# A SwiGLU feed-forward kernel: the last 96 rows of the down-projection in row quarters of the array

## The chip, the cores and the metric

The kernel runs on one core of one Trainium2 chip. A core has a matmul engine (TensorE, an array of 128 x 128 cells), VectorE, ScalarE, GpSimd, SyncE and 16 DMA engines. The metric is the device time of one execution in microseconds (us). The kernel before takes 121.23 us, the median of three runs (120.81 to 121.36).

## The reference

x has 2048 tokens of 512 numbers; the weights are 512 x 1376, 512 x 1376 and 1376 x 512; all is bf16.

```python
g = silu(x @ w_gate)
u = x @ w_up
return (g * u) @ w_down
```

1376 = 10 x 128 + 96. The hidden dimension therefore has ten full blocks of 128 and a rest of 96.

## The kernel before

Everything stays in the core's own memory: x transposed (`xT_sb`), both input weights (`w_sb`), w_down (`wd_sb`), and h = silu(gate) * up, transposed, hidden rows on partitions (`hT_sb`, eleven blocks; block 10 holds the last 96 rows). A planner at lines 116 to 211 writes down all groups of matmuls in order, and gives each group the next of eight accumulator banks in turn. The engines wait for each other by counters: TensorE counts groups (`s_P`), ScalarE and VectorE count their operations (`s_A`, `s_D`).

The order on TensorE (`on_tensor`):

- six warming matmuls (L290) and eight transposes of the first rows of x (L297);
- for each of four chunks of 512 tokens, ten pairs of groups G and U (gate and up for one hidden block, four matmuls each of 128 x 128 weights and 512 tokens, L282). ScalarE takes silu of G, VectorE multiplies it by U and writes h (L242). After the ten pairs follows one group X (L316), four matmuls with 64 columns of gate and 64 of others, which gives 32 of the last 96 rows of h;
- two groups Y (L327), each for two chunks: sixteen matmuls in all whose weights have 64 columns, in pairs, one in the left and one in the right half of the array's columns. They give the other 64 of the last 96 rows, which VectorE multiplies and writes to `hT_sb[0:64, 10]`;
- sixteen output tiles of 128 tokens, groups O (L344): each is eleven matmuls into one bank, ten over 128 hidden rows and one over the last 96. The last tile is in two banks, of 384 and 128 output columns, so that its first part can be copied and stored earlier.

VectorE copies each finished output bank to one of three buffers `o_sb` (L246; ScalarE copies the 384 columns of the last tile, L235), and SyncE stores the buffer (L218). SyncE also issues nearly all loads, at the start (lines 99 to 112); the stores stand behind them in its queue. A wait of SyncE holds back all that follows on it. ScalarE has nothing to do between the last silu and the copy of the last tile.

A group may start when the bank's former group, eight groups before, has been read (`free`). A load that has to be there is waited for once (`need`).

Of the kernel before, what the change touches and what calls it, by code (L numbers as in the profile page):

```python
# [6 lines left out]
BF16 = mybir.dt.bfloat16  # L7
# [5 lines left out]
def bass_standalone__swiglu_ffn__prompt_kernel(nc, x, w_gate, w_up, w_down, out):  # L13
    _, S, D = x.shape
    F = w_gate.shape[1]
    P = 128
    KD = D // P
    NFF = F // P
    NFT = NFF + 1
    F_LAST = F - NFF * P  # L20
    SC = 512
    NSC = S // SC
    TPC = SC // P
    NST = S // P
    LASTA = 384
    HT = SC // 2
    NB = 8
    NSG = 4
    NOS = 3
    assert D == 512 and S % SC == 0 and KD == 4 and F_LAST == 96 and NSC % 2 == 0  # L30

    xf = x[0]
# [8 lines left out]
    with ExitStack() as es:  # L41
        sb = lambda name, shape, dt: es.enter_context(nc.sbuf_tensor(name, shape, dt))
        ps = lambda name, shape, dt: es.enter_context(nc.psum_tensor(name, shape, dt))
        sem = lambda name: es.enter_context(nc.semaphore(name))

        xT_sb = sb("xT_sb", [P, KD, S], BF16)
        w_sb = sb("w_sb", [P, KD, WTOT], BF16)
        wd_sb = sb("wd_sb", [P, NFT, D], BF16)
        hT_sb = sb("hT_sb", [P, NFT, S], BF16)
        adummy = sb("act_dummy", [P, 8], FP32)  # L50
        sg_sb = [sb(f"sg_sb{i}", [P, SC], FP32) for i in range(NSG)]
        sgx_sb = [sb(f"sgx_sb{c}", [P, SC], FP32) for c in range(NSC)]
# [6 lines left out]
        s_P = sem("s_P")  # L59
        s_A = sem("s_A")  # L60
        s_D = sem("s_D")
        s_I = sem("s_I")
        s_out = [sem(f"s_out{i}") for i in range(NOS)]
        loads = {}

        def load_sem(name):
            loads[name] = sem(f"s_{name}")
            return loads[name]
# [23 lines left out]
        def load_up(eng, a, b):  # L92
            load_w(eng, f"wu{a}", w_up, UPH, a * P, min(b * P, F - 32))

        def loads_on_scalar(act):
            load_gate(act, *slabs[0])
            load_up(act, *slabs[0])

        def loads_on_sync(sp):
            for t in range(TPC // 2):  # L100
                sp.dma_start(x0_sb[:, t, :], xf[t * P:(t + 1) * P, :]).then_inc(load_sem(f"t{t}"), 16)
            load_x(sp, "x0b", HT, SC)
            for a, b in slabs[1:]:
                load_gate(sp, a, b)
                load_up(sp, a, b)
            load_w(sp, "wut", w_up, F - (F - 32), F - 32, F)
            for c in range(1, NSC):
                load_x(sp, f"x{c}", c * SC, (c + 1) * SC)
            sp.dma_start(
                wd_sb[:, 0:NFF, :], w_down[0:NFF * P, :].rearrange("(k p) d -> p k d", p=P)  # L110
            ).then_inc(load_sem("wd"), 16)
            sp.dma_start(wd_sb[0:F_LAST, NFF, :], w_down[NFF * P:F, :]).then_inc(load_sem("wdt"), 16)

        groups = []
        n_read = {"A": 0, "D": 0}
# [7 lines left out]
        def add_op(eng, g, **what):  # L125
            n_read[eng] += 1
            op = dict(g=g, at=n_read[eng], **what)
            (act_ops if eng == "A" else dve_ops).append(op)
            g["readers"].append((eng, op["at"]))
            return op  # L130
# [3 lines left out]
        h_ready = {}  # L134
# [18 lines left out]

        y_after = {}
        t_ready = {}

        def plan_x(c):
            g = add_group("X", c=c)
            y0, y1 = yblk(c)
            add_op("A", g, kind="silu", out=sgx_sb[c][96:128, :], src=g["bank"][64:96, :], free=0)  # L160
            a = add_op("A", g, kind="silu", out=sgy_sb[c][y0:y1, :], src=g["bank"][0:64, :], free=0)
            add_op(
                "D", g, kind="mul", out=hT_sb[64:96, NFF, c * SC:(c + 1) * SC],
                a=sgx_sb[c][96:128, :], b=g["bank"][96:128, :], after=a["at"] - 1,
            )
            y_after[c] = a["at"]
# [13 lines left out]
        for t in range(TPC // 2):  # L180
            for half, eng in enumerate("AD"):
                g = add_group("T", t=t, k0=2 * half)
                op = add_op(
                    eng, g, kind="copy", stored=(s_I, 0),
                    out=xT_sb[:, 2 * half:2 * half + 2, t * P:(t + 1) * P],
                    src=g["bank"][:, 0:2 * P].rearrange("p (k t) -> p k t", k=2),
                )
                x0_ready.append((2 * half, eng, op["at"]))
        n_T = len(groups)
# [9 lines left out]
        for t in range(NST):  # L199
            ob = t % NOS  # L200
            need = 16 * n_store[ob]
            halves = [(0, D)] if t < NST - 1 else [(0, LASTA), (LASTA, D)]
            for c0, c1 in halves:
                g = add_group("O", t=t, c0=c0, c1=c1)
                eng = "A" if len(halves) == 2 and c0 == 0 else "D"
                op = add_op(
                    eng, g, kind="copy", out=o_sb[ob][:, c0:c1], src=g["bank"][:, 0:c1 - c0],
                    stored=(s_out[ob], need),
                )
# [3 lines left out]

        def on_sync(sp):
            loads_on_sync(sp)
            for t, c0, c1, ob, eng, n in stores:
                sp.wait_ge(s_A if eng == "A" else s_D, n)
                sp.dma_start(of[t * P:(t + 1) * P, c0:c1], o_sb[ob][:, c0:c1]).then_inc(s_out[ob], 16)  # L218
            for i in range(NOS):
                sp.wait_ge(s_out[i], 16 * n_store[i])  # L220

        def on_scalar(act):
            loads_on_scalar(act)
            act.activation(adummy[:, 0:4], zero_c, ACT.Silu)  # L224
            for op in act_ops:
                act.wait_ge(s_P, op["g"]["at"] + 1)
                if op["kind"] == "silu":
                    if op["free"]:
                        act.wait_ge(s_D, op["free"])
                    fn = ACT.Silu  # L230
                else:
                    if op["stored"][1]:
                        act.wait_ge(*op["stored"])
                    fn = ACT.Copy
                act.activation(op["out"], op["src"], fn).then_inc(s_A, 1)  # L235
# [13 lines left out]
        def on_tensor(pe):  # L249
            landed = set()  # L250

            def need(name):
                if name not in landed:
                    pe.wait_ge(loads[name], 16)
                    landed.add(name)
# [3 lines left out]
            def after(eng, n):  # L259
                if n > read[eng]:  # L260
                    pe.wait_ge(s_A if eng == "A" else s_D, n)
                    read[eng] = n

            def free(g):
                if g["at"] >= NB:
                    for eng, n in groups[g["at"] - NB]["readers"]:
                        after(eng, n)
# [35 lines left out]
            for n0, n1 in ((0, HT), (HT, SC)):  # L303
                for g in groups[n_T:n_T + 2]:
                    gu_matmuls(g, n0, n1)
            for g in groups[n_T + 2:]:
                free(g)
                kind = g["kind"]
                if kind in "GU":
                    gu_matmuls(g, 0, SC)  # L310
                elif kind == "X":
                    c = g["c"]
                    need(f"wg{slab_of[NFF]}")
                    need("wut")
                    for dk in range(KD):
                        ins = pe.matmul(  # L316
                            g["bank"][:, :], lhsT=w_sb[:, dk, XC0:XC0 + P],
                            rhs=xT_sb[:, dk, c * SC:(c + 1) * SC],
                            start=(dk == 0), stop=(dk == KD - 1),
                        )  # L320
                    ins.then_inc(s_P, 1)
                elif kind == "Y":
                    need(f"wu{slab_of[NFF]}")
                    for dk in range(KD):
                        for c in (2 * g["pi"], 2 * g["pi"] + 1):
                            y0, y1 = yblk(c)
                            ins = pe.matmul(  # L327
                                g["bank"][y0:y1, :], lhsT=w_sb[:, dk, YC0:YC0 + 64],
                                rhs=xT_sb[:, dk, c * SC:(c + 1) * SC],
                                start=(dk == 0), stop=(dk == KD - 1),  # L330
                                tile_position=(0, y0), skip_group_check=True,
                            )
                    ins.then_inc(s_P, 1)
                else:
                    t, c0, c1 = g["t"], g["c0"], g["c1"]
                    c = t // TPC
                    need("wd")
                    after("D", h_ready[c])
                    for fk in range(NFT):
                        K = P if fk < NFF else F_LAST  # L340
                        if fk == NFF:
                            need("wdt")
                            after("D", t_ready[c])
                        ins = pe.matmul(  # L344
                            g["bank"][:, 0:c1 - c0], lhsT=hT_sb[0:K, fk, t * P:(t + 1) * P],
                            rhs=wd_sb[0:K, fk, c0:c1], start=(fk == 0), stop=(fk == NFT - 1),
                        )
                    ins.then_inc(s_P, 1)

        nc.gpsimd.affine_select(  # L350
            ident[:, :], ones_w, pattern=[[-1, P]], compare_op=ALU.is_equal, fill=0.0, base=0,
# [34 lines left out]
```

## Time and profile before

| | |
|---|---|
| time of the profiled execution | 121.29 us |
| its span, first to last instruction | 120.0 us |
| median of three runs | 121.23 us |
| TensorE matmuls (L282, L316, L327, L344) in the profile | 328, 16, 16, 187 |
| VectorE copy of an output bank (L246) | 0.69 us |
| ScalarE silu of a bank (L235) | 0.60 us |
| store of a 128 KB output tile, issue to landing | 1.7 us |
| granted TensorE clock | 1.0 |

The span runs from the first instruction to the last, the time of the execution a little more. "Busy" of TensorE is from the start of a matmul to its modelled end; a matmul begins well before its predecessor has ended, so the mean duration of one (379 ns at 512 columns) is longer than the step from start to start, and it is the step that counts for the time. The weight load of a matmul is an instruction of its own (PEld), which in this kernel mostly runs beside the matmul before it.

### The profile page before, as it was taken

How to read it: one execution, taken by the hardware profiler on the slowest of the kernel's cores; microseconds unless marked ns; L12 is line 12 of the kernel's file. 1: busy time of each engine (PE TensorE's matmuls, PEld its weight loads, DVE VectorE, ACT ScalarE, POOL GpSimd, SP SyncE). 2: the span in 40 equal slices, each digit the busy share in tenths (PEclk: the TensorE clock that was granted, in tenths of full speed). 3: DMA queues.
4: the chain of work that ended last, by engine and by line, in shares of the span. 5: the costliest groups of instructions: out<-in, count | busy, mean ns of one | idle time of the engine just before them, and what ended most of it. 6: DMA issues, size and time to landing. Idle time of an engine off the chain costs nothing.

```text
span 120.0 us, 1415 instructions
## 1 busy us (share of the span) xinstructions
PE 117.0 (97%) x561; PEld 53.9 (45%) x561; DVE 44.5 (37%) x66; ACT 31.1 (26%) x53; POOL 0.5 (0%) x5
## 2 busy tenths in 40 slices
PE   7899999999999999999999999999999999999993
PEld 2564444444444444444444444344444444444452
DVE  0224433444434444334444334466233224222420
ACT  3333233262333272333262333230000000000001
POOL 1000000000000000000000000000000000000000
DMA  3999999930000000000000000000211121111112
GB/s 89 231 306 372 287 218 182 302 127 0 0 0 0 0 0 5 0 0 5 0 0 0 0 5 0 0 0 0 87 44 44 52 85 44 44 66 66 44 44 87
DMA packets 17254, 8.51 MB, mean 71 GB/s; under 512 B 10496, under 2 KB 17248, under 8 KB 17248
## 3 DMA queue, kind: packets, MB, share of 16 engines
q1 hardware_dynamic: 16192, 8.16, 25.4%
q10 hardware_dynamic: 1056, 0.26, 1.0%
q8 instruction: 4, 0.07, 0.3%
q14 instruction: 2, 0.02, 0.0%
HBM read 4.49 MB, written 2.10 MB: 55 GB/s over the span
## 4 chain that ended last, share of the span: by engine, by line
PE 97%; ACT 0%; DVE 0%; issue 0%
PE bank L282 58%; PE bank L344 32%; PE bank L316 3%; PE bank L290 2%; PE bank L327 2%; PE bank L297 1%; ACT xT_sb L235 0%; DVE o_sb L246 0%
## 5 line engine op out<-in xcount | busy, mean ns | idle before, releaser
L282 PE MATMUL bank<-xT_sb,w_sb 128*128 128x512 bf16 (+1 forms) x328 | 70.2, 376 | 0.4 <-ACT xT_sb L235 0.4
L282 PEld LDWEIGHTS bank<-xT_sb,w_sb 128*128 128x128 bf16 x328 | 32.2, 98 | 37.7 <-issue 0.6
L242 DVE TENSOR_TENSOR hT_sb<-sg_sb,bank 128x512 bf16<-128x512 f32 x40 | 27.5, 688 | 40.8 <-PE bank L282 37.6
L344 PE MATMUL bank<-wd_sb,hT_sb 128*128 128x512 bf16 (+4 forms) x187 | 38.3, 367 | 0.0
L235 ACT ACTIVATE sg_sb<-bank 128x512 f32<-128x512 f32 x40 | 23.8, 596 | 41.6 <-PE bank L282 41.6
L344 PEld LDWEIGHTS bank<-wd_sb,hT_sb 128*128 128x128 bf16 (+1 forms) x187 | 17.8, 98 | 20.7 <-DVE hT_sb L242 0.4
L246 DVE CAST o_sb<-bank 128x512 bf16<-128x512 f32 (+1 forms) x16 | 10.7, 667 | 25.4 <-PE bank L344 25.3
L235 ACT ACTIVATE o_sb<-bank 128x384 bf16<-128x384 f32 x1 | 0.5, 490 | 38.2 <-PE bank L344 38.2
L316 PE MATMUL bank<-xT_sb,w_sb 128*128 128x512 bf16 x16 | 4.1, 379 | 0.0
L242 DVE TENSOR_TENSOR hT_sb<-sgx_sb,bank 32x512 bf16<-32x512 f32 x4 | 2.8, 692 | 3.5 <-ACT sgx_sb L235 3.5
L290 PE MATMUL bank<-const-bfloat16-1.0 128*128 128x512 bf16 x6 | 2.7, 623 | 0.8 <-PEq L371 0.8
L235 ACT ACTIVATE sgx_sb<-bank 32x512 f32<-32x512 f32 x4 | 2.3, 587 | 4.5 <-PE bank L316 4.5
L242 DVE TENSOR_TENSOR hT_sb<-sgy_sb,bank 64x512 bf16<-64x512 f32 x4 | 2.7, 685 | 0.1
L316 PEld LDWEIGHTS bank<-xT_sb,w_sb 128*128 128x128 bf16 x16 | 1.6, 98 | 1.9
L246 DVE CAST xT_sb<-bank 128x256 bf16<-128x256 f32 x2 | 0.8, 424 | 4.2 <-PE bank L297 4.0
L235 ACT ACTIVATE sgy_sb<-bank 64x512 f32<-64x512 f32 x4 | 2.4, 589 | 0.1
L327 PE MATMUL bank<-xT_sb,w_sb 128*64 128x512 bf16 x16 | 1.9, 382 | 0.0
L224 ACT ACT_TABLE_LOAD x1 | 1.3, 1283 | 1.9 <-issue 1.9
L290 PEld LDWEIGHTS bank<-const-bfloat16-1.0 128*128 128x128 bf16 x6 | 0.7, 133 | 1.9 <-issue 1.9
L327 PEld LDWEIGHTS bank<-xT_sb,w_sb 128*64 128x64 bf16 x16 | 0.8, 109 | 1.0 <-DVE hT_sb L242 0.4
L297 PE MATMUL bank<-ident,x_sb 128*128 128x128 bf16 x8 | 1.2, 309 | 0.0
L297 PEld LDWEIGHTS bank<-ident,x_sb 128*128 128x128 bf16 x8 | 0.8, 133 | 0.8 <-issue 0.5
(7 smaller groups left out, 1.7 us busy)
## 6 DMA issues: line engine op xcount, KB each, us to landing
out_dram<-o_sb SPq DMA_DIRECT2D x15, 128.0 KB, 1.7
wd_sb<-in_w_down_dram SPq DMA_DIRECT2D x1, 1280.0 KB, 6.9
w_sb<-in_w_gate_dram SPq DMA_DIRECT2D x1, 480.0 KB, 5.5
w_sb<-in_w_up_dram SPq DMA_DIRECT2D x1, 448.0 KB, 6.1
w_sb<-in_w_gate_dram SPq DMA_DIRECT2D x1, 384.0 KB, 4.6
w_sb<-in_w_up_dram SPq DMA_DIRECT2D x1, 384.0 KB, 5.1
x_sb<-in_x_dram SPq DMA_DIRECT2D x2, 128.0 KB, 2.5
w_sb<-in_w_gate_dram SPq DMA_DIRECT2D x1, 256.0 KB, 3.9
```

The source lines that it names most:

```text
L224: act.activation(adummy[:, 0:4], zero_c, ACT.Silu)
L235: act.activation(op["out"], op["src"], fn).then_inc(s_A, 1)
L242: ins = dve.tensor_tensor(op["out"], op["a"], op["b"], ALU.mult)
L246: ins = dve.tensor_copy(op["out"], op["src"])
L282: ins = pe.matmul(g["bank"][:, n0:n1], lhsT=w_sb[:, dk, col:col + P], rhs=xT_sb[:, dk, c * SC + n0:c * SC + n1], start=(dk == 0), stop=(dk ...
L290: pe.matmul(banks[NB - 1][:, :], lhsT=ones_w, rhs=ones_m, start=True, stop=True)
L297: ins = pe.matmul(g["bank"][:, i * P:(i + 1) * P], lhsT=x0_sb[:, g["t"], k * P:(k + 1) * P], rhs=ident[:, :], start=True, stop=True,)
L316: ins = pe.matmul(g["bank"][:, :], lhsT=w_sb[:, dk, XC0:XC0 + P], rhs=xT_sb[:, dk, c * SC:(c + 1) * SC], start=(dk == 0), stop=(dk == KD - 1),
L327: ins = pe.matmul(g["bank"][y0:y1, :], lhsT=w_sb[:, dk, YC0:YC0 + 64], rhs=xT_sb[:, dk, c * SC:(c + 1) * SC], start=(dk == 0), stop=(dk == ...
L344: ins = pe.matmul(g["bank"][:, 0:c1 - c0], lhsT=hT_sb[0:K, fk, t * P:(t + 1) * P], rhs=wd_sb[0:K, fk, c0:c1], start=(fk == 0), stop=(fk == ...
```

## The change

The 96-row matmuls of the output tiles are replaced, all but the very last one of 128 columns. The 96 rows are three pieces of 32. For four tiles at once, four matmuls of 32 rows, each in its own quarter of the array's rows and into its own bank, go one after the other: quarter r takes tile r; three such packs make up the 96 rows of four tiles. A matmul in a quarter reads weights and data from the partitions of that quarter, so the rows have to lie in all four quarters:

- `wdr_sb` holds the last 96 rows of w_down four times, by four loads;
- `hr_sb` holds the 32 rows of piece i for tile r on the partitions of quarter r. `spread` issues four DMAs for one piece and one pair of chunks, 24 in all. SyncE issues pieces 2 and 0 (16 DMAs) ahead of all stores, each after a wait for the VectorE multiplies that write them; ScalarE issues piece 1 (8 DMAs) ahead of its only output copy.

The order of the output groups, for each pair of chunks (eight tiles): 40 matmuls of the ten full blocks of four tiles (the banks stay open), the 12 quarter matmuls that close these four banks, the 12 that open the next four, and then the 40 matmuls that finish those, bank by bank. The closing of four banks is told once, by an increment of four. The last 128 columns of the last tile follow by themselves, as before. There are six output buffers instead of three, and the load of the last 96 rows into `wd_sb` brings only the 128 columns that the last group needs.

```diff
-    NOS = 3
+    NOS = 6
+    R = 32
+    NPC = 3
...
+        wdr_sb = sb("wdr_sb", [P, NPC, D], BF16)
+        hr_sb = sb("hr_sb", [P, NSC, NPC, P], BF16)
...
+        def spread(eng, pi, i):
+            for r in range(TPC):
+                tok = slice(2 * pi * SC, (2 * pi + 2) * SC)
+                eng.dma_start(
+                    hr_sb[R * r:R * (r + 1), 2 * pi:2 * pi + 2, i, :],
+                    hT_sb[R * i:R * (i + 1), NFF, tok].rearrange("p (c t) -> p c t", c=2)[:, :, r * P:(r + 1) * P],
+                ).then_inc(s_hr[pi], 16)
...
-            sp.dma_start(wd_sb[0:F_LAST, NFF, :], w_down[NFF * P:F, :]).then_inc(load_sem("wdt"), 16)
+            load_sem("wdr")
+            for r in range(TPC):
+                sp.dma_start(
+                    wdr_sb[R * r:R * (r + 1), :, :], w_down[NFF * P:F, :].rearrange("(i p) d -> p i d", p=R)
+                ).then_inc(loads["wdr"], 16)
+            sp.dma_start(wd_sb[0:F_LAST, NFF, LASTA:D], w_down[NFF * P:F, LASTA:D]).then_inc(load_sem("wdt"), 16)
...
         def on_sync(sp):
             loads_on_sync(sp)
+            for pi in range(NSC // 2):
+                sp.wait_ge(s_D, x_ready[2 * pi + 1])
+                spread(sp, pi, 2)
+            for pi in range(NSC // 2):
+                sp.wait_ge(s_D, t_ready[2 * pi + 1])
+                spread(sp, pi, 0)
             for t, c0, c1, ob, eng, n in stores:
...
             for op in act_ops:
+                if op["g"]["kind"] == "O":
+                    for pi in range(NSC // 2):
+                        act.wait_ge(s_D, t_ready[2 * pi + 1])
+                        spread(act, pi, 1)
...
+            def strips(c, gs, first, last):
+                pe.wait_ge(s_hr[c // 2], 16 * NPC * TPC)
+                for i in range(NPC):
+                    for r, g in enumerate(gs):
+                        c0, c1 = g["c0"], g["c1"]
                         ins = pe.matmul(
-                            g["bank"][:, 0:c1 - c0], lhsT=hT_sb[0:K, fk, t * P:(t + 1) * P],
-                            rhs=wd_sb[0:K, fk, c0:c1], start=(fk == 0), stop=(fk == NFT - 1),
+                            g["bank"][:, 0:c1 - c0], lhsT=hr_sb[R * r:R * (r + 1), c, i, :],
+                            rhs=wdr_sb[R * r:R * (r + 1), i, c0:c1],
+                            start=first and i == 0, stop=last and i == NPC - 1,
+                            tile_position=(R * r, 0), skip_group_check=True,
                         )
-                    ins.then_inc(s_P, 1)
+                return ins
+
+            og = [g for g in groups if g["kind"] == "O"]
+            for pi in range(NSC // 2):
+                ga = og[2 * pi * TPC:(2 * pi + 1) * TPC]
+                gb = og[(2 * pi + 1) * TPC:(2 * pi + 2) * TPC]
+                for g in ga:
+                    free(g)
+                    mains(g, True, False)
+                for g in gb:
+                    free(g)
+                if "wdr" not in landed:
+                    pe.wait_ge(loads["wdr"], 16 * TPC)
+                    landed.add("wdr")
+                strips(2 * pi, ga, False, True).then_inc(s_P, TPC)
+                strips(2 * pi + 1, gb, True, False)
+                for g in gb:
+                    mains(g, False, True).then_inc(s_P, 1)
+            g = og[-1]
+            free(g)
+            mains(g, True, False)
+            need("wdt")
+            after("D", t_ready[NSC - 1])
+            pe.matmul(
+                g["bank"][:, 0:g["c1"] - g["c0"]], lhsT=hT_sb[0:F_LAST, NFF, g["t"] * P:(g["t"] + 1) * P],
+                rhs=wd_sb[0:F_LAST, NFF, g["c0"]:g["c1"]],
+                start=False, stop=True,
+            ).then_inc(s_P, 1)
```

`mains(g, first, last)` issues the ten full-block matmuls of one group, after waiting for `wd` and for the h of the chunk; its `start` and `stop` say whether the bank is opened by its first matmul and closed by its last.

## The prediction

> **What bounds the kernel now.** I read the page first, for the share of each engine, then the chain of work that ended last, then the groups with their shapes kept apart, then the timeline around the two places where the array's shape changes.
>
> The page's first part:
>
> ```profile
> PE 117.0 (97%) x561; PEld 53.9 (45%) x561; DVE 44.5 (37%) x66; ACT 31.1 (26%) x53; POOL 0.5 (0%) x5
> ```
>
> TensorE works in 97% of the span, everything else in under half of it. The chain in order of time (start, length, what; us):
>
> ```profile
> 59.98 17.27 PE bank L282 x80
> 77.24 0.86 PE bank L316 x4
> 78.11 1.85 PE bank L327 x16
> 79.95 38.21 PE bank L344 x187
> 118.16 0.02 issue
> 118.19 0.29 DVE o_sb L246
> ```
>
> The chain hardly leaves TensorE: what shortens or lengthens its stream moves the end one for one. 17.27 / 80 = 0.2159 us is the pace of a 512-column matmul. The 187 matmuls of the down-projection run without a hole at that pace. Its groups, shapes kept apart (busy, mean ns of one):
>
> ```profile
> L344 PE MATMUL bank<-wd_sb,hT_sb 128*128 128x512 bf16 x150 | 34.8, 379 | 0.0
> L344 PE MATMUL bank<-wd_sb,hT_sb 96*128 96x512 bf16 x15 | 5.7, 381 | 0.0
> L327 PE MATMUL bank<-xT_sb,w_sb 128*64 128x512 bf16 x16 | 1.9, 382 | 0.0
> L344 PEld LDWEIGHTS bank<-wd_sb,hT_sb 96*128 96x128 bf16 x17 | 1.7, 98 | 1.8
> L327 PEld LDWEIGHTS bank<-xT_sb,w_sb 128*64 128x64 bf16 x16 | 0.8, 109 | 1.0 <-DVE hT_sb L242 0.4
> ```
>
> A 96-row matmul lasts as long as a 128-row one (381 against 379 ns): a quarter of the array idles in it. The 379 ns are start to modelled end; the next one starts after 216. The 16 half-width matmuls of L327 were busy for 1.9 us together: 8 pairs, not 16 in a row. So two column halves of the array do run side by side here. Row quarters do not occur in this trace.
>
> **What is removed.** Of the 17 matmuls over the last 96 rows, 16 go: fifteen of 512 columns and one of 384. The pace of 384 columns comes from the timeline of TensorE:
>
> ```profile
> 115.58 1.79 PE L344 MATMUL bank<-wd_sb,hT_sb 128*128 128x384 bf16 x10
> ```
>
> The last of these ten starts at 115.58 + 1.79 - 0.33 (its duration) = 117.04, so nine steps took 1.46 us, 0.162 each. Removed: 15 x 0.2159 + 0.162 = **3.40 us**, all on the path.
>
> **What is added on TensorE.** 48 quarter matmuls (32 rows), in 12 packs of four: 3 pieces of 32 rows x 4 sections of four banks. A pack cannot be faster than the 512 columns that each member streams, 0.216 us; if the four did not overlap at all it would be 4 x 0.2159 = 0.864. Nearest row: the pairs of L327. Their first starts at 78.04 and the last ends at 79.95, so it started at 79.57 (382 ns each); of these 1.53 us, 7 x 0.2159 = 1.51 are the steps between eight pairs and 0.02 is how much the second member lags. A pair thus costs one matmul's pace. Four members need four weight loads per pack, where the pair needs two. The nearest row for a dense row of loads is the tail of 128 columns:
>
> ```profile
> 117.59 0.56 PE L344 MATMUL bank<-wd_sb,hT_sb 128*128 128x128 bf16 x7
> ```
>
> (0.56 - 0.22) / 6 = 57 ns for a load with its matmul. Four of those make 0.228 us, hardly above 0.216. I take 0.216: 12 x 0.2159 = **2.59 us**; at 0.228 it is 2.74. The change of matmuls alone is 3.40 - 2.59 = 0.81 us less.
>
> **What the changes of shape cost.** The two closing-and-opening sections stand together, so the array changes to quarters twice and back twice. The trace has one such change each way, into and out of L327's halves:
>
> ```profile
> 77.08 1.03 PE L316 MATMUL bank<-xT_sb,w_sb 128*128 128x512 bf16 x4
> 77.08 0.53 PEld L316 LDWEIGHTS bank<-xT_sb,w_sb 128*128 128x128 bf16 x3
> 77.28 0.69 DVE L242 TENSOR_TENSOR hT_sb<-sg_sb,bank 128x512 bf16<-128x512 f32 x1 [1.04 <-PE bank L282]
> 78.03 0.14 PEld L327 LDWEIGHTS bank<-xT_sb,w_sb 128*64 128x64 bf16 x4 [0.42 <-DVE hT_sb L242]
> 78.04 0.41 PE L327 MATMUL bank<-xT_sb,w_sb 128*64 128x512 bf16 x2
> ...
> 79.88 0.76 PEld L344 LDWEIGHTS bank<-wd_sb,hT_sb 128*128 128x128 bf16 x5 [0.41 <-DVE hT_sb L242]
> 79.89 1.04 PE L344 MATMUL bank<-wd_sb,hT_sb 128*128 128x512 bf16 x4
> ```
>
> The last L316 starts at 77.08 + 1.03 - 0.38 = 77.73; at pace its successor would start at 77.95 and starts at 78.04: 0.09 late. On the way back, 79.57 + 0.216 = 79.79 against 79.89: 0.10 late. The loads tell why: elsewhere a load runs ahead beside the matmul before it; here it starts 0.01 us ahead of its own matmul. The page names VectorE's multiply as what ended the wait, but what the halves wait for is the read of a bank used eight groups before, a multiply three pairs (some 5 us) earlier. So I take the 0.09 and 0.10 as the price of the change of shape: 2 x (0.09 + 0.10) = 0.39 us, plus the lag of a pack's fourth member, 3 x 0.02 per section, 0.12 us in all. Together **0.51 us**. Bounds: nothing, if quarters need no such pause; 0.38 us each (a matmul's whole duration before the next begins), 1.5 us. I stay with 0.1, the only change of shape measured here.
>
> **What the copies of h cost.** 24 small DMAs copy the last 96 rows of h to the four quarters, 16 issued by SyncE, 8 by ScalarE; four loads of the last rows of w_down replace one. The stores queue behind the copies on SyncE. Issue rows of SyncE (start, length):
>
> ```profile
> 19.10 0.58 SPq L109 DMA_DIRECT2D wd_sb<-in_w_down_dram  x1
> 19.73 0.69 SPq L112 DMA_DIRECT2D wd_sb<-in_w_down_dram  x1
> ...
> 118.50 0.38 SPq L218 DMA_DIRECT2D out_dram<-o_sb  x1
> ```
>
> The loads are issued before 25 us and wanted after 80: nothing. The copies for the first two sections: four wait for the multiplies of the X groups, the last of which ends at 78.83 + 0.69 = 79.52, and four more on SyncE for the Y multiplies, at 79.56 + 1.40 = 80.96. (Four for the first pair of the X pieces went long before; here the second pair's stand in front.) Eight issues at 0.38 to 0.69 from 79.5 are done by 82.6 to 85.0; landing takes 1.7 (store) to 2.5 us (small x load) by the page, so 84.3 to 87.5. First wanted: after 40 matmuls, 79.89 + 40 x 0.2159 = 88.53. So it is hidden, with 1 to 4 us to spare. ScalarE issues its eight in a stretch of 38 us in which it waits only for the last tile. What stands behind the waits on SyncE is the first store, and its data now come after 89 us. Later copies have 17 us more.
>
> **Banks and the end.** A section now hands four banks over at once: VectorE needs 4 x 0.69 = 2.8 us for them, in which TensorE runs a section of packs and then the 2.16 us of the next bank; the four banks are wanted again about 8 us later. Six output buffers instead of three let the four copies go without a store between them. The last bank keeps its eleven matmuls of 128 columns and the same copy and store: no change behind TensorE.
>
> **Sum.** -3.40 + 2.59 + 0.51 = -0.30 us. The profiled execution took 121.29 us (span 120.0, 1.3 around it); the median of the three runs is 121.23. 121.29 - 0.30 = 120.99: I forecast **121.0**, 0.2% below the median, inside the 0.5% (0.6 us) that a measurement can tell from no change. With the packs at 0.228 it is 121.1.
>
> One statement speaks against the sum. The Trainium skill, "TensorE: Matmul & The Clock Gate", section "Measured speedup vs the span model", gives four 32-row tiles of 512 columns a speedup of 3.07, not 4. As an estimate from that page, a pack would be 4 x 0.2159 / 3.07 = 0.281 us, twelve 3.38, and the kernel 121.8. The pairs of L327 reach 2.0 here, so I keep the trace's pace; no row here shows quarters.
>
> **Rivals.**
>
> *Quarters change shape for nothing (faster).* If the pause of L327 belongs to halves of columns (their load lasts 109 ns for 64 columns, the full one 98 for 128, so they load otherwise), only the 0.12 us of lag stay: -0.69 us, 120.6; without lag 120.5. Against it: the pause is there in both directions, into and out of the halves.
>
> *The loads of a quarter do not run ahead (slower).* If a load into the quarter that is in use waits for that quarter's matmul, each pack shows the 0.1 us that a load not run ahead costs at the change of shape: 12 x 0.1 = +1.2 us, so 121.29 - 0.30 + 1.2 = 122.2. It makes the kernel slower by over 0.5% from (0.6 + 0.3) / 12 = 75 ns per pack on. Against it: in L327 four loads lie within 0.14 us, ahead of the second pair, and the pairs keep the pace of 0.216. For it: eight loads in flight, not four, and no row of quarters.
> The skill's same page, section "The mechanism", says that a load overlaps a running matmul only where their row groups differ; the pairs of L327 use all rows, and their loads overlap, so the trace does not bear that out here.
>
> *The quarters do not run side by side.* Two at a time: 24 x 0.2159 = 5.18, so +2.3 us, 123.6; one at a time 10.4 us, 128.8. For it only that the trace has no row quarter; it would mean that the packs do not do what they are for.
>
> *Rows of h come late.* With all issues at 0.93 us (the longest issue of a weight load in the trace) eight end at 87.0, land at 89.5, 0.9 us late: 121.9. The short issue rows speak against it, since each copy is small.
>
> **Chances.** Forecast (packs 0.216 to 0.228, pauses near 0.1; 120.8 to 121.4): 0.47. No pause: 0.26. Loads exposed: 0.15. Not side by side: 0.07. Late rows: 0.05. So faster by over 0.5%: 0.26, within: 0.47, slower: 0.27. The range from 120.5 to 122.2 takes in the free and the exposed case and leaves out the not-side-by-side one and the ends of the others.
>
> **What would show it.** Twelve packs with starts 0.216 apart, four members within some 0.06 us; a load that starts just ahead of its matmul and a start about 0.1 us late at each of four places; no wait on a DMA at the first quarter matmul near 88.5 us; the span shorter by 0.3. A step of 0.28 or more between packs makes me wrong upwards, matmuls at pace across the change of shape downwards.

## The result, and the profile after

The changed kernel takes 120.82 us (median of 22 runs, 120.45 to 121.47) where the kernel before, run beside it, takes 121.16. The medians differ by 0.34 us; the ratio is 0.9969, 95% interval 0.9956 to 0.9983. (A ratio compares fast runs alone, here without one slow run of 123.48 us, and is not the plain quotient of the medians.) A second comparison, told below, gave 0.9994 (0.9968 to 1.0020). Both intervals hold 0.2 to 0.3% less, and the second also holds no gain at all. The forecast was 0.2% less, and 121.0 us: 0.18 more than measured, mostly as it was counted from one execution of 121.29. The difference is below the 0.5% that was called the limit of a measurement here, so the traces have to carry the explanation.

The page of the changed kernel, first part, and its chain of work in order of time (start, length, what; us):

```profile
PE 116.1 (97%) x593; PEld 53.0 (44%) x593; DVE 44.0 (37%) x66; ACT 31.1 (26%) x53; POOL 0.5 (0%) x5
```

```profile
77.66 1.85 PE bank L359 x16
79.51 8.74 PE bank L373 x40
88.25 1.41 PE bank L385 x24
89.65 17.37 PE bank L373 x80
107.03 1.40 PE bank L385 x21
108.43 8.77 PE bank L373 x50
117.19 0.07 PE bank L414
117.27 0.02 issue
117.29 0.29 DVE o_sb L278
```

The one piece of 38.21 us (L344) has become six. The two of L385 are the quarter matmuls: 24 in 1.4 us, where 24 in a row would take 5.2 (the chain counts 21 in the second piece; it holds 24 too, three of them of 384 columns). Such a piece, from the change to quarters to the change back, is called a stay. From the start of the first full output matmul to the start of the last matmul, the down-projection took 79.89 to 117.93 before and takes 79.44 to 117.03 now: 38.04 against 37.59, **0.45 us less**. (That it starts 0.45 us earlier as well has nothing to do with the change: the first 88 gate and up matmuls, which are the same, took 17.95 us in one profiled execution and 17.48 in the other, since some of the first ones, of 256 columns, went at half pace in the former, 0.213 us from start to start where 0.109 is usual. A version below that equals the changed kernel up to there took 18.15. That is why spans of single executions, 120.0 and 119.3, are not compared here, but stretches.)

The timeline around the first stay in quarters (start, length, engine, line, in how many):

```profile
87.22 1.03 PE L373 MATMUL bank<-wd_sb,hT_sb 128*128 128x512 bf16 x4
87.44 0.31 PEld L373 LDWEIGHTS bank<-wd_sb,hT_sb 128*128 128x128 bf16 x2
88.17 0.98 PEld L385 LDWEIGHTS bank<-wdr_sb,hr_sb 32*128 32x128 bf16 x24 [0.42 <-issue]
88.18 1.48 PE L385 MATMUL bank<-wdr_sb,hr_sb 32*128 32x512 bf16 x24
89.06 1.89 DVE L278 CAST o_sb<-bank 128x512 bf16<-128x512 f32 x3 [7.11 <-PE bank L385]
89.58 0.98 PEld L373 LDWEIGHTS bank<-wd_sb,hT_sb 128*128 128x128 bf16 x6 [0.42 <-issue]
89.59 1.25 PE L373 MATMUL bank<-wd_sb,hT_sb 128*128 128x512 bf16 x5
```

This is the picture that L327 gave before: at each change of shape the first weight load starts 0.01 us ahead of its own matmul instead of beside the one before it. The last full matmul starts at 87.87, the first quarter at 88.18: 0.312 us where 0.216 is the pace, **0.10 late**. The last quarter starts at 89.28, the next full one at 89.59: 0.306, **0.09 late**. No wait on a DMA stands there; the idle time of the load is "issue".

The end holds what the forecast did not have. The last store is issued at 117.61 and lands 1.5 us later:

```profile
117.61 0.39 SPq L246 DMA_DIRECT2D out_dram<-o_sb  x1
```

```profile
out_dram<-o_sb SPq DMA_DIRECT2D x1, 32.0 KB, 1.5
```

The landing is at 119.11, but the span ends at 119.30. In the kernel before, issue 118.50, landing 120.01, end 120.03. What stands behind the landing are SyncE's closing waits for the output buffers, before and after (how many; shortest, median and longest in ns; first and last start):

```profile
L220 SPq EVENT_SEMAPHORE  x2: 17/522/1027, 118.9 to 119.0; - x2
```

```profile
L248 SPq EVENT_SEMAPHORE  x3: 28/28/28, 119.1 to 119.3; - x3
```

The records join the waits for two buffers in one instruction, and not in the order of the program: before, buffer 1 alone, then 2 with 0; now 3 with 2, 4 with 1, 5 with 0. The last store is from buffer 0 before and from buffer 3 now. So the wait that the last store releases was the last instruction before (1027 ns long, to 120.03), and is the first of three now: they end at 119.16, 119.23 and 119.30. **0.17 us came back at the end**. Sum of the two stretches: -0.45 + 0.17 = -0.28 us.

### The profile page after: what moved, and what is told of

The parts are those of the page before. It is cut to its first block, busy times and chain, and to the rows that moved or that the text cites. A ratio compares the mean times of both kernels' runs of the same rounds, so it can differ in the third digit from the quotient of the medians.

```text
span 119.3 us, 1509 instructions
## 1 busy us (share of the span) xinstructions
PE 116.1 (97%) x593; PEld 53.0 (44%) x593; DVE 44.0 (37%) x66; ACT 31.1 (26%) x53; POOL 0.5 (0%) x5
## 4 chain that ended last, share of the span: by engine, by line
PE 97%; ACT 0%; DVE 0%; issue 0%
PE bank L314 58%; PE bank L373 29%; PE bank L348 3%; PE bank L385 2%; PE bank L322 2%; PE bank L359 2%; PE bank L329 1%; ACT xT_sb L267 0%; DVE o_sb L278 0%; PE bank L414 0%
## 5 line engine op out<-in xcount | busy, mean ns | idle before, releaser
L373 PE MATMUL bank<-wd_sb,hT_sb 128*128 128x512 bf16 (+2 forms) x170 | 35.1, 367 | 0.0
L373 PEld LDWEIGHTS bank<-wd_sb,hT_sb 128*128 128x128 bf16 x170 | 16.0, 98 | 19.2 <-issue 0.8
L278 DVE CAST o_sb<-bank 128x512 bf16<-128x512 f32 (+1 forms) x16 | 10.1, 663 | 25.5 <-PE bank L385 15.8
L385 PE MATMUL bank<-wdr_sb,hr_sb 32*128 32x512 bf16 (+1 forms) x48 | 2.9, 373 | 0.0
L385 PEld LDWEIGHTS bank<-wdr_sb,hr_sb 32*128 32x128 bf16 x48 | 1.1, 93 | 1.7 <-issue 0.8
```

Source lines behind the costliest of these rows:

```text
L278: ins = dve.tensor_copy(op["out"], op["src"])
L373: ins = pe.matmul(g["bank"][:, 0:c1 - c0], lhsT=hT_sb[:, fk, t * P:(t + 1) * P], rhs=wd_sb[:, fk, c0:c1], start=first and fk == 0, stop=la ...
L385: ins = pe.matmul(g["bank"][:, 0:c1 - c0], lhsT=hr_sb[R * r:R * (r + 1), c, i, :], rhs=wdr_sb[R * r:R * (r + 1), i, c0:c1], start=first an ...
```

## The experiments

Theory: the packs run at the pace of one full matmul, and each change of shape stops TensorE for about 0.1 us. Rivals: changes of shape are free, and the late starts have another cause; the loads of the quarters are exposed. Times are medians; ratios are to the kernel before, run on the same chip.

**Two more stays in quarters.**

```diff
-                strips(2 * pi + 1, gb, True, False)
-                for g in gb:
+                mains(gb[0], True, False)
+                strips(2 * pi + 1, gb, True, False).then_inc(s_P, 1)
+                for g in gb[1:]:
                     mains(g, False, True).then_inc(s_P, 1)
```

(and `start` is not set for the first tile of the second section.)

> Each of the two places with quarter matmuls is parted in two by the ten full matmuls of the fifth tile, so that the array changes shape eight times instead of four; number and kind of matmuls stay. Theory (a change of shape stops TensorE for 0.10 us on the way in and 0.09 on the way out, about 0.21 with the slow first steps): two more stays, +0.42 us, 121.2 us, ratio to the kernel before about 1.000. Rival (the late starts belong to something met once per pair of chunks, such as the wait for the copies of h or for the banks, and a change of shape is free): as the changed kernel, 120.8, ratio 0.997.

Measured: 121.29 us, ratio 1.0017 (0.9998 to 1.0035). Its chain:

```profile
88.22 0.76 PE bank L385 x12
88.98 2.26 PE bank L373 x10
91.25 0.76 PE bank L385 x12
```

The down-projection takes 38.02 us from first to last start against 37.59: +0.43 for four more changes of shape, with the same matmuls. The whole gain of the change is gone in this stretch. The rival of free changes falls.

**Every pack twice.**

```diff
-                for i in range(NPC):
+                for i in list(range(NPC)) * 2:
```

(`start` and `stop` are set in the first and the last of the six rounds.)

> Every pack of quarter matmuls is run twice in the same stay (the last 96 rows are then added twice in all tiles but for the last 128 columns). Twelve more packs, no further change of shape. Theory (a pack costs one matmul's pace, 0.2155 us, its loads are hidden): +2.59 us, 123.4, ratio 1.0185. Rival (the weight loads of a quarter are exposed for 0.1 us per pack): +3.8, 124.6, ratio 1.028. The Trainium skill's speedup of 3.07 (TensorE: Matmul & The Clock Gate, Measured speedup vs the span model) would make it +3.4, 124.2.

Measured: 123.41 us, ratio 1.0189 (1.0164 to 1.0214). Its stays:

```profile
88.62 2.70 PE bank L387 x48
91.32 17.37 PE bank L373 x80
108.70 2.70 PE bank L387 x42
```

48 quarter matmuls in 2.70 us, 24 in 1.41: 1.29 for six packs, 0.215 each. From first to last start the down-projection is 2.59 us longer for twelve packs. So four quarters give the work of four matmuls in the time of one, not of 1.3 (the speedup of 3.07 cited above would need 0.281), and the loads are hidden. The rival of exposed loads falls.

**No quarter matmuls at all.** `strips` is not called; the full matmuls close the banks.

> All 48 quarter matmuls are left out (the last 96 rows are missing in all tiles but for the last 128 columns); the copies of h and the wait for them stay. Theory: the changed kernel less twelve packs and four changes of shape, 2.59 + 0.41 = 3.0 us, 117.8, ratio 0.973. Rival (the changes of shape cost nothing): 118.2, ratio 0.976. TensorE's last row should pass from full matmul to full matmul at 0.216 us all through the down-projection.

Measured: 117.98 us, ratio 0.9735 (0.9712 to 0.9758). The time alone does not part 0.973 from 0.976. The chain does:

```profile
80.04 34.66 PE bank L373 x170
114.70 0.07 PE bank L414
```

34.57 us from first to last start, 3.02 less than the changed kernel's 37.59. Twelve packs account for 2.59; 0.43 is left for four changes of shape. The wait for the copies of h still stands where the quarter matmuls were, and no step there is longer than 0.216 us: so it is the change of shape, and not this wait, that makes the starts late. Against the kernel before (38.04) the stretch is 3.47 us shorter: that is what the change removes, measured without what it adds.

**Quarter by quarter instead of pack by pack.**

```diff
-                for i in range(NPC):
-                    for r, g in enumerate(gs):
+                for r, g in enumerate(gs):
+                    for i in range(NPC):
```

> The same 48 quarter matmuls in another order: the three pieces of one quarter one after the other, then the next quarter. Theory (matmuls start in program order, and one in a quarter that is in use waits and holds back those behind it): only the last of one quarter and the first of the next run side by side, 17 steps per stay instead of 6, 2 x 11 x 0.2155 = +4.7 us, 125.6, ratio 1.037. Rival (TensorE picks those whose quarter is free): as the changed kernel, 120.8, ratio 0.997. Rival (matmuls of two quarters overlap only within a pack that starts together): 24 steps per stay, +7.8 us, 128.6.

Measured: 120.81 us, ratio 0.9979 (0.9963 to 0.9995). The theory of this experiment fell, by 4.8 us:

```profile
88.44 1.43 PE bank L385 x24
89.87 17.37 PE bank L373 x80
107.24 1.42 PE bank L385 x21
```

The stays are as short as before. TensorE started matmuls out of the program's order. This can be seen in the second stay, where the fourth tile has 384 columns: its three matmuls are the last three of the stay in the program. The groups of TensorE that run in the window from 108.06 to 108.07 us:

```profile
L385 PE MATMUL bank<-wdr_sb,hr_sb 32*128 32x512 bf16 x6 | 0.6, 374 | 0.0
L385 PE MATMUL bank<-wdr_sb,hr_sb 32*128 32x384 bf16 x2 | 0.5, 321 | 0.0
```

And the timeline from 108.52 to 108.58:

```profile
108.27 0.39 PE L385 MATMUL bank<-wdr_sb,hr_sb 32*128 32x512 bf16 x3
```

Two matmuls of 384 columns are running (started at 107.86 and 108.03) when matmuls of 512 that stand ahead of them in the program have yet to start; the last to start are three of 512. The changed kernel itself shows it, too: in the last two packs of its second stay the member of 384 columns, last in the program, starts 0.04 and 0.10 us ahead of the other three.

**The same with twelve in a row for each quarter.** Quarter by quarter, and each piece four times (`for n in range(4 * NPC)` with `i = n % NPC`; `start` and `stop` at the first and the last of the twelve).

> Quarter by quarter as in the former experiment, and each piece four times (the last 96 rows are added four times in all tiles but for the last 128 columns): twelve matmuls of one quarter stand one after the other in the program, so the fourth quarter's first is 36 matmuls and as many weight loads behind the first quarter's first. Theory (TensorE starts what has a free quarter, however far behind it stands): 48 packs at 0.2155 instead of 12, 120.8 + 7.8 = 128.6, ratio 1.061. Rival (it looks only some matmuls ahead, far enough for the nine of the former experiment and not for 36): in between, up to 177 steps instead of 48, 156, ratio 1.29.

Measured: 169.58 us, ratio 1.4008 (1.3930 to 1.4086). The theory fell and the rival was too low. Engines by stretch (start:end, total; then busy time and number of instructions of PE, PEld, DVE, ACT and POOL; then the granted clock, the share of the DMA engines and GB/s):

```profile
88.50:90.25 1.75, 1.75 (x9) 0.75 (x9) 0.00 (x0) 0.00 (x0) 0.00 (x0) 1.00 0.00 0
90.25:92.00 1.75, 1.75 (x14) 0.80 (x13) 0.00 (x0) 0.00 (x0) 0.00 (x0) 1.00 0.00 0
92.50:96.00 3.50, 3.50 (x16) 1.25 (x14) 0.00 (x0) 0.00 (x0) 0.00 (x0) 0.51 0.02 5
112.00:113.50 1.50, 1.50 (x5) 0.31 (x3) 0.00 (x0) 0.00 (x0) 0.00 (x0) 0.50 0.00 0
118.00:120.00 2.00, 2.00 (x11) 0.88 (x9) 0.53 (x2) 0.00 (x0) 0.00 (x0) 1.00 0.19 66
```

Eight matmuls of the first quarter start one by one, 0.216 apart; the first of the second quarter starts at 90.26, with the ninth (90.25). So three of the first quarter were waiting when the program went on to the next: a quarter seems to hold three matmuls in wait, enough for the former experiment and not for this one. (It is no limit of three for all quarters together: in the former experiment two of each of three quarters, six in all, were waiting when the fourth quarter's first started.) Then, at 92.54, the granted clock fell to one half, although TensorE was never idle, and came back at 116.44, 2.7 us after full matmuls had begun again. With the steps of 0.427 us that this gives, the first stay takes 25 us. The second stay repeats it: 132.41 to 155.87 us, with half the clock from 136.92 to 160.81, and all four executions show a mean clock of 0.86 to 0.87. The 128.6 and the 156 us of the forecasts had reckoned with the full clock.

**The closing waits in another order.**

```diff
-            for i in range(NOS):
+            for i in [4, 5, 0, 1, 2, 3]:
                 sp.wait_ge(s_out[i], 16 * n_store[i])
```

> SyncE's six closing waits in another order, so that the buffer stored last (number 3) is waited for last; nothing else changes. Theory (in the changed kernel two waits that are long fulfilled stand behind the landing of the last store, 0.07 us each, and the span ends 0.19 us after the landing instead of 0.02): -0.15 us against the changed kernel, 120.67, ratio to the kernel before 0.9958. Rival (those waits overlap the end of the program that follows anyway): 120.82, ratio 0.997, with the last record still nearer to the landing.

Measured: 120.62 us, ratio 0.9953 (0.9934 to 0.9972). The last store's row:

```profile
117.99 0.39 SPq L246 DMA_DIRECT2D out_dram<-o_sb  x1
```

It lands at 119.50 and the span ends at 119.54: 0.04 us behind it instead of 0.19. The down-projection is unchanged (37.59). The rival, that the end of the program hides those waits, falls as well: what an execution takes beyond its span is 1.30 us on average with either order.

The changed kernel and this one once more, side by side:

> The changed kernel as it is, beside the next one on one chip: ratio to the kernel before 0.997 again, 120.8.

> The changed kernel with the last store waited for last, once more. Theory (the two waits behind the last landing cost 0.15 us): 0.15 us less than the changed kernel beside it, ratio 0.9955. Rival (the former 0.2 us were chance): as the changed kernel, 0.997.

Measured: the changed kernel 121.09 us, ratio 0.9994 (0.9968 to 1.0020); with the other order 120.67, ratio 0.9975 (0.9954 to 0.9996). The ratios differ by 0.19% (0.2 us; the medians by 0.42), in the first comparison, where each had its own runs of the kernel before, by 0.16%; the intervals overlap, so the size rests on the trace, where the 0.15 us between landing and end are gone both times (landing 119.24, end 119.28 here). Each time this version has a lower median than every other kernel that was run beside it.

**Three output buffers.** `NOS = 3`.

> The changed kernel with three output buffers as before. Of the four copies that follow a closing of four banks, the last must wait for a store to land. Theory (TensorE wants those banks some 8 us later, so the wait is hidden, and there are fewer closing waits): the changed kernel less 0.1 to 0.17 us, 120.65 to 120.7, ratio 0.9958. Rival (VectorE's late copies hold back banks): over 120.9, with waits of TensorE on VectorE in the down-projection.

Measured: 120.84 us, ratio 0.9968 (0.9946 to 0.9990). Undecided in the time: the interval holds the forecast 0.9958 and the changed kernel's 0.9969. In the trace the span ends 0.02 us behind the landing, and VectorE does wait for stores:

```profile
DVE o_sb L278 <- DMA out_dram<-o_sb: 2.9, 3, 1.6
```

Three waits, 2.9 us, and the down-projection still takes 37.59 us: hidden, as TensorE wants the banks later. The six buffers are not needed for the gain. By its trace this version should take as long as the one with the other order of waits, which was run beside it; its median is 0.22 us higher, and the two intervals overlap. The trace does not show why.

**All copies of h by SyncE.** `spread(sp, pi, 1)` behind `spread(sp, pi, 0)`; ScalarE issues none.

> All 24 copies of h are issued by SyncE, so that eight more issues of 0.64 us stand in its queue. The last copy for the first pair should land at 87.9 us instead of 85.4, TensorE wants it at 88.1. Theory (2.8 us of cover, of which 2.6 go): no difference, 120.8, ratio 0.997; at most 0.1 us of waiting at the first quarter matmul. Rival (the copies are near the path already): 0.5 us or more, ratio over 1.001.

Measured: 120.88 us, ratio 0.9976 (0.9949 to 1.0004). SyncE's queue:

```profile
79.59 12.73 SPq L105 DMA_DIRECT2D hr_sb<-hT_sb  x20
92.36 2.62 SPq L247 DMA_DIRECT2D out_dram<-o_sb  x3
```

The last copy for the first pair lands at 88.42, the first quarter matmul starts at 88.66, 0.312 us after the full one, as before: no wait. In the changed kernel that copy lands at 85.38 for a start at 88.18. The cover of 2.8 us is real, and this experiment uses nearly all of it.

**The kernel before with 128 rows.** The last block's rows 96 to 127 are zeros in both operands, `K = P` throughout.

> The kernel before, with the last block's 96 rows filled up to 128 by rows of zeros that GpSimd writes at the start, so that all 187 matmuls of the down-projection have 128 rows. Theory (the step from a 96-row matmul to a 128-row one takes 220 ns instead of 216): the 0.06 us in the trace go, all steps 216 ns; too little to be told in the time, ratio 0.9995. Rival (the 4 ns belong to the change of bank or of the group's end): the steps stay at 220 ns.

Measured: 121.14 us, ratio 0.9993 (0.9970 to 1.0017), which tells nothing by itself, as expected. In the trace of the kernel before, the step from a 96-row matmul to the next 128-row one is 219.9 ns on average (14 steps); any other step to 512 columns is 215.8 to 216.0; here those 14 are 215.9. The chain's piece of 38.21 us is

```profile
79.89 38.13 PE bank L347 x187
```

0.08 us shorter, in one profiled execution each. The 4 ns belong to the change from 96 rows to 128; the rival, that they belong to the change of bank, falls.

## Why the prediction was right, and where it was not

- *What is removed*, 3.40 us: right, and 0.06 us more, the sixteen steps out of a 96-row matmul that take some 4 ns longer, which the prediction had not seen: 3.46, where the version without quarter matmuls shows 3.47.
- *What is added on TensorE*, 2.59 us: right. Pack follows pack by 0.2155 us; doubling them costs 2.59.
- *What the changes of shape cost*: 0.09 in and 0.10 out were taken from the halves of L327; the quarters take 0.10 and 0.09. Four more changes cost 0.43. The lag of the fourth member was misread: 0.06 us per stay were put down where it is 0.01. In L327's pairs the second member starts 0.003 us after the first; the 0.02 that the prediction took for its lag was the first step after the change, 0.240 us instead of 0.216, which comes once in a stay and not in each pack. In sum two stays cost 0.41 us above their packs, not 0.51. From the last full start to the next full one a stay takes 1.719 and 1.716 us; less an ordinary step each that is 3.00 for both, against 3.46 removed.
- *What the copies of h cost*, nothing: right. An issue takes 0.6 us, a landing 1.8; the cover is 2.8 us, within the 1 to 4 that were given.
- *Banks*: right, also with only three buffers.
- *The end*: **wrong**. "The same copy and store: no change behind TensorE" looked at the work and not at the waits that close the program. With six buffers the last tile's buffer is number 3 instead of number 0; its wait is the first of the three recorded instead of the last, and two that have long been fulfilled stand behind the landing: 0.17 us. The version with the other order takes them away.

So the forecast of -0.30 us holds against -0.28 in the two stretches and -0.34 in the medians, but partly by luck: the work on TensorE gained 0.45, one and a half times the forecast, and the end gave 0.17 back.

Of the rivals, free changes of shape (-0.69) and exposed loads (+0.9) were shown wrong by the parted and the doubled packs; quarters that do not run side by side and late rows do not occur. What stays open is the size of the time difference itself: two comparisons give 0.3 and 0.1%, and no more than 0.2 to 0.3% can be claimed. In the traces the down-projection takes 37.59 us in all six executions that have the changed kernel's order of matmuls; of the kernel before there is one trace, with 38.04.

## What to carry to other kernels

Packing row quarters costs one matmul's pace per pack of four and about 0.2 us for each stay, so a stay should hold many packs: here one matmul in four is saved (0.22 us per section), and with one section per stay the gain would be nil. Where a kernel ends with waits for several buffers, the buffer stored last is waited for last, and the trace is asked whether its wait is the last one recorded. When two kernels differ by less than single executions scatter, compare stretches of the trace that hold the change, and their ends.

## What the runs showed of the hardware that was not expected

- Matmuls in different row quarters start out of program order: nine matmuls of three quarters were no hindrance for the fourth. The Trainium skill ("TensorE: Matmul & The Clock Gate", "The mechanism") says that matmuls start and end in program order; the 384-column rows above show otherwise for quarters. A counter raised by the last quarter matmul in the program therefore tells of the others only if that one also comes last on the engine; pack by pack, members of equal length start within 0.01 us in the program's order, a shorter one up to 0.10 us ahead of it.
- A quarter seems to hold some three matmuls in wait: with twelve in a row the next quarter began at the ninth.
- TensorE working without a pause, but mostly in one quarter of its rows, lost half its clock 4.0 us after it began (1.0 to 0.5, 88.52 to 92.54 us) and got it back 2.7 us after full matmuls resumed; in the second stay it was 4.5 and 4.9 us. The stretches between the changes, 23.89, 20.48 and 23.89 us, are 7, 6 and 7 times 3.413.
- A wait of SyncE that is already fulfilled costs 0.07 us at the end of the program (one instruction, which asks two counters).
